# One block of a fused attention and expert kernel: ScalarE's queue put in another order

## The chip, the core and the metric

The kernel runs on one core of a Trainium2 chip. The core has a matrix engine (TensorE, PE in the profile), a vector engine (VectorE, DVE), an activation engine (ScalarE, ACT), GpSimd (POOL) and SyncE (SP), which here only issues DMA transfers. Each engine has its own list of instructions, works through it in order, and waits at an instruction until the semaphores that this instruction names have been raised by other engines or by a landed transfer. The metric is the device time of one launch in microseconds (us). Lower is better.

## What is computed

Three steps follow each other, on 2304 tokens of width 512:

```
scores = scale * q_c @ k_c.T                # attention in chunks of 64, 8 heads
attn   = exp(scores - max) / (sum + 1e-09)
x      = attn @ v_c
h = x @ w_in                                # first MLP, 512 -> 2048 -> 512
x = (h * clip(h + 3, 0, 6) / 6) @ w_out
...                                         # then top 2 of 8 experts, 512 -> 1024 -> 512 each
```

## The kernel before

**Precision by parts.** TensorE works on 32-bit values in a rounded format. To keep accuracy each operand is held as a rounded part ("hi") and a remainder ("lo"), and a product takes three passes: hi by hi, hi by lo, lo by hi. ScalarE makes each hi (a copy that rounds), VectorE makes the matching lo (value minus hi).

**Blocks and units.** The first MLP is done in five blocks of 4, 3, 4, 4 and 3 token tiles of 128 (`BT`). A block runs over `U1 = 16` units of 128 hidden columns. In unit u TensorE makes the first product (`mlp_s1`, L310, 12 matmuls), then the second product of the unit before (`mlp_o`, L322, 12 matmuls). Between the two stand four instructions that are called the chain of the activation here: ScalarE's relu (`mlp_r`, L351), VectorE's minimum and product (L352), ScalarE's copy g hi (`mlp_g`, L356), VectorE's remainder g lo (`mlp_lo`, L364).

**The first block does more.** `block0` is the only block in which the MLP's weights come as raw 64-bit words and have to be made into hi and lo. Each unit has two halves, one of `w_in` and one of `w_out`, of 512 KB raw. In unit u the half a = 2u+4 (unit u+2's `w_in`) and the half b = 2u+3 (unit u+1's `w_out`) are made: VectorE's shift `conv_1` (L160), merge `conv_2` (L167) and merge `conv_3` (L174), then ScalarE's copy `conv_hi` (L184), then VectorE's remainder `conv_lo` (L191). Raw halves land in three buffers (and for some early ones in spare room); `load_next` has SyncE load a further half when a `conv_3` has freed a buffer (L150). The remainder of half b is made one unit later, just behind L352: the code calls that half `late`.

In the same block the attention of tiles 4, 5 and 6 is done, each spread over four units, from unit 2, 6 and 10 on. I number these four units k = 0 to 3. In k = 0 the scores are there (`att_sc`); VectorE takes the maximum (`att_mx`, L211, L215) and ScalarE four of eight exponentials (`att_e`, L226). In k = 1 come the other four exponentials, VectorE's reciprocal of the sums (`att_r`, L236, L237) and four of eight scalings by it (`att_ns`, L250). In k = 2 come the other scalings. In k = 3 TensorE transposes (`att_pt`, L257), ScalarE copies that (`att_at`, L265), TensorE multiplies by v (`att_xo`, L278), and the result is split into hi (`att_hi`, L288) and lo (`att_lo`, L291). The next tile's q, k, v (768 KB) are loaded when `att_xo` is done (L119).

**What sets the order.** TensorE, VectorE and ScalarE are under a manual schedule: each engine's list is the order of the Python calls below. SyncE's transfers are placed by the scheduler.

Of the kernel before, what the change touches and what calls it, by code (L numbers as in the profile page):

```python
# [52 lines left out]
def tile_kernel(ctx, tc, qkv, w1u, w2u, wg, noise, out):  # L53
# [51 lines left out]
    late = tc.tile_pool(name="late", bufs=1)  # L105
# [56 lines left out]
    def conv_2(s):  # L162
        if s >= 2 * U1:
            return
        hi32 = st["raw64", s].rearrange("p (n c) -> p n c", c=2)[:, :, 1]
        u = st["u", s]
        nc.vector.scalar_tensor_tensor(u, hi32, -0x40000000, u, op0=ALU.bitwise_and, op1=ALU.bitwise_or)  # L167

    def conv_3(s):
        if s >= 2 * U1:  # L170
            return
        lo32 = st.pop(("raw64", s)).rearrange("p (n c) -> p n c", c=2)[:, :, 0]
        u = st["u", s]
        nc.vector.scalar_tensor_tensor(u, lo32, 29, u, op0=ALU.logical_shift_right, op1=ALU.bitwise_or)  # L174

    def load_next(*halves):
        for s in halves:
            load64(s + 7 if s < 10 else s + 3 if s >= 14 else -1)

    def conv_hi(s):  # L180
        if s >= 2 * U1:
            return
        j, h = divmod(s, 2)
        nc.scalar.activation(st["w", "m", j][:, 0, h * DM:(h + 1) * DM], st["u", s].bitcast(F32), AF.Copy)  # L184

    def conv_lo(s):
        if s >= 2 * U1:
            return
        j, h = divmod(s, 2)
        hi, lo = (st["w", "m", j][:, i, h * DM:(h + 1) * DM] for i in range(2))  # L190
        nc.vector.tensor_tensor(lo, st.pop(("u", s)).bitcast(F32), hi.bitcast(F32), op=ALU.subtract)  # L191
# [39 lines left out]
    def att_r(t, eng=None):  # L231
        eng = eng or nc.vector
        sm, su, mx, acts = st["att", t]
        if not acts:
            nc.vector.tensor_reduce(su, sm, axis=AX.X, op=ALU.add)
        eng.tensor_scalar(su, su, 1e-9, None, op0=ALU.add)  # L236
        nc.vector.reciprocal(su, su)  # L237
# [9 lines left out]
    def att_ns(t, heads):  # L247
        sm, su, mx, acts = st["att", t]
        for h in heads:
            nc.scalar.activation(sm[:, h], sm[:, h], AF.Copy, scale=su[:, h])  # L250
# [9 lines left out]
    def att_at(t, at, dve=False):  # L260
        dst, src = at.rearrange("p k n -> p (k n)"), st.pop(("pt", t))
        if dve:
            nc.vector.tensor_copy(dst, src)
        else:
            nc.scalar.activation(dst, src, AF.Copy)  # L265
        st["attT", t] = at
# [81 lines left out]
    def mlp_r(b, u):  # L348
        n = BT[b] * P
        r = work.tile([P, DM], F32, tag="r", bufs=2, name="r")[:, :n]  # L350
        nc.scalar.activation(r, st["h", b], AF.Relu, bias=b3)  # L351
        nc.vector.scalar_tensor_tensor(r, r, 6.0, st["h", b], op0=ALU.min, op1=ALU.mult)  # L352
        st["r", b] = r

    def mlp_g(b, u):
        nc.scalar.activation(st["g", b, u][:, 0], st["r", b], AF.Copy)  # L356
# [537 lines left out]
    def block0():  # L894
        nonlocal prev
        n0, lag = st.get("tick", 0), 2
        for i in range(BT[1]):
            k = n0 + 7 * (4 * i + lag)
            t = LT + i
            at(ticks, k + 3, att_sc, t)  # L900
            at(ticks, k + 20, att_pt, t)
            at(ticks, k + 24, att_xo, t)
        late = []
        for u in range(U1):
            t, k = LT + (u - lag) // 4, ((u - lag) % 4 if lag <= u < lag + 4 * BT[1] else None)
            b, a = 2 * u + 3, 2 * u + 4
            mlp_s1(0, u, gtile(), 0)
            mlp_r(0, u)
            if k == 3:
                att_at(t, at_[0])  # L910
            mlp_g(0, u)
            if u == 0:
                conv_3(1), conv_hi(1), conv_lo(2)
                load_next(1, 2)
                late = [1]
            else:
                conv_lo(*late)
            for pb, v in prev:
                mlp_o(pb, v)
            prev = [(0, u)]  # L920
            if k == 1:
                att_e(t, range(4, 8))
            elif k == 2:
                att_ns(t, range(4, 8))
            conv_1(a), conv_2(a)
            mlp_lo(0, u)
            if u == 0:
                conv_lo(*late)
            conv_1(b)
            conv_3(a), conv_hi(a)  # L930
            conv_2(b)
            if k == 0:
                att_mx(t, True)
            elif k == 1:
                att_r(t)
            elif k == 3:
                att_hi(t)
            conv_3(b), conv_hi(b)
            conv_lo(a)
            if k == 0:  # L940
                att_e(t, range(4))
            elif k == 1:
                att_ns(t, range(4))
            elif k == 3:
                att_lo(t)
                if t + 2 < NTILE:
                    load_tile(t + 2, bufs[4 + t % 2])
            late = [b]
            load_next(b, a)

    nxt = {"u": U1}
# [185 lines left out]
```

## Time and profile before

| what | us |
|---|---|
| median of three runs (lowest, highest) | 950.94 (950.82, 953.96) |
| the profiled execution's own time | 942.9 |
| its span, first to last instruction | 941.1 |
| TensorE busy in the span | 910.5 |
| VectorE busy | 480.6 |
| ScalarE busy | 332.4 |

The profiled execution is a launch of its own, so its rows add up to 942.9 and not to the median. Busy time is summed over the whole span; the first block's units lie between about 20 and 131 us of it, and what bounds them is read from that stretch alone.

### The profile page before, as it was taken

The numbers are of one execution on the slowest core, as the hardware profiler recorded it, in microseconds if no ns is written. First come the engines' busy times: TensorE is split into PE (matmuls) and PEld (weight loads), VectorE is DVE, ScalarE is ACT, GpSimd is POOL, SyncE is SP. The second block draws the span as 40 slices with busy tenths as digits, with TensorE's granted clock in tenths as the row PEclk, the third lists the DMA queues.
The fourth block names the chain that finished last, engine by engine and source line by source line (L and its number), as shares of the span: only waits on it lengthen the run. The fifth ranks groups of instructions, "written<-read, shape, count | busy, mean of one in ns | idle before, by whom it ended". The sixth has DMA issues, their size and how long they took to land. (4 is left out here: it accounts for less than half of the span.)

```text
span 941.1 us, 14415 instructions
## 1 busy us (share of the span) xinstructions
PE 910.5 (97%) x5804; PEld 766.3 (81%) x5804; DVE 480.6 (51%) x912; ACT 332.4 (35%) x642; POOL 231.8 (25%) x214
## 2 busy tenths in 40 slices
PE   7988899999999999999999999999999999999996
PEld 4666678888777777788988898889898988888885
DVE  7888875463445344536553455444545444441321
ACT  5455543333323222344551443333333333321210
POOL 1000000011001000032202435763655446332311
PEclk9999999999999999999999999999999999999998
DMA  9625449322200610013640764563736445240412
GB/s 341 226 85 156 148 131 346 94 68 69 68 26 13 181 41 1 1 58 83 186 146 2 156 170 129 122 153 93 160 99 132 118 118 141 69 54 20 54 23 34
DMA packets 49916, 101.49 MB, mean 108 GB/s; under 512 B 17040, under 2 KB 23056, under 8 KB 49840
## 3 DMA queue, kind: packets, MB, share of 16 engines
q1 hardware_dynamic: 38736, 80.38, 27.2%
q0 software_dynamic: 11104, 20.10, 11.8%
q8 instruction: 47, 0.77, 0.4%
q14 instruction: 29, 0.24, 0.1%
HBM read 77.66 MB, written 22.75 MB: 107 GB/s over the span
## 5 line engine op out<-in xcount | busy, mean ns | idle before, releaser
L322 PE MATMUL bp<-w,g 128*128 128x512 f32 (+1 forms) x1812 | 456.7, 398 | 4.7 <-ACT g L356 3.4
L322 PEld LDWEIGHTS bp<-w,g 128*128 128x128 f32 (+1 forms) x1812 | 328.8, 186 | 81.2 <-ACT g L356 5.4
L310 PE MATMUL bp<-Xa,w 128*128 128x304 f32 (+3 forms) x1344 | 241.2, 330 | 2.1 <-ACT Xa L288 1.3
L310 PEld LDWEIGHTS bp<-Xa,w 128*128 128x128 f32 x1344 | 210.1, 188 | 24.8 <-ACT Xa L288 1.4
L583 POOL DMA_INDIRECT xrq<-x2d,iq x114 | 119.2, 1045 | 96.1 <-DVE iq L577 34.8
L626 DVE SCALAR_TENSOR_TENSOR g<-bp,g 128x304 fp32r<-128x304 f32 (+2 forms) x128 | 60.3, 471 | 130.9 <-ACT g L625 130.8
L139 DVE TENSOR_TENSOR w<-raw,w 128x1024 fp32r<-128x1024 f32 x64 | 78.4, 1226 | 89.2 <-ACT w L138 89.2
L548 POOL DMA_INDIRECT table<-pay,slot x36 | 36.2, 1006 | 339.3 <-DVE slot L545 329.9
L625 ACT ACTIVATE g<-bp 128x304 fp32r<-128x304 f32 (+2 forms) x128 | 54.2, 424 | 168.7 <-PE bp L310 168.5
L310 PE MATMUL bp<-Xb,w 128*128 128x384 f32 (+1 forms) x480 | 106.1, 366 | 0.0
L352 DVE SCALAR_TENSOR_TENSOR r<-r,bp 128x512 f32<-128x512 f32 (+1 forms) x80 | 50.7, 634 | 105.7 <-ACT r L351 105.3
L310 PE MATMUL bp<-Xe,w 128*128 128x304 f32 (+1 forms) x672 | 102.7, 308 | 0.0
L310 PEld LDWEIGHTS bp<-Xe,w 128*128 128x128 f32 x672 | 99.8, 188 | 3.3
L310 PEld LDWEIGHTS bp<-Xb,w 128*128 128x128 f32 x480 | 85.2, 188 | 12.5 <-issue 1.8
L653 POOL DMA_INDIRECT out_dram<-arena,tab x40 | 62.6, 1564 | 123.6 <-DVE arena L650 100.2
L138 ACT ACTIVATE w<-raw 128x1024 fp32r<-128x1024 f32 x64 | 67.7, 1058 | 59.3 <-PE bp L322 58.6
L351 ACT ACTIVATE r<-bp,b 128x512 f32<-128x512 f32 (+1 forms) x80 | 51.3, 641 | 105.6 <-PE bp L310 105.6
L364 DVE TENSOR_TENSOR g<-r,g 128x512 fp32r<-128x512 f32 (+1 forms) x80 | 50.9, 637 | 39.7 <-ACT g L356 39.5
L356 ACT ACTIVATE g<-r 128x512 fp32r<-128x512 f32 (+1 forms) x80 | 47.1, 589 | 57.3 <-DVE r L352 57.3
L184 ACT ACTIVATE w<-u 128x512 fp32r<-128x512 f32 x32 | 20.2, 632 | 47.0 <-DVE u L174 47.0
L401 DVE STREAM_TRANSPOSE arena<-xrq 128x512 f32<-128x512 f32 (+1 forms) x30 | 31.4, 1045 | 0.0
L767 POOL MEMSET zero<- 128x1024 f32 x1 | 1.0, 953 | 110.3 <-DMA arena<-in_qkv_dram 110.3
(150 smaller groups left out, 479.5 us busy)
## 6 DMA issues: line engine op xcount, KB each, us to landing
raw<-in_w2u_dram SPq DMA_DIRECT2D x64, 512.0 KB, 3.6
raw<-in_w1u_dram SPq DMA_DIRECT2D x24, 512.0 KB, 4.5
arena<-in_qkv_dram SPq DMA_DIRECT2D x14, 768.0 KB, 11.6
out_dram<-zero SPq DMA_DIRECT2D x4, 1536.0 KB, 10.7
rawx<-in_w1u_dram SPq DMA_DIRECT2D x8, 512.0 KB, 3.7
x2d<-x SPq DMA_DIRECT2D x15, 256.0 KB, 2.2
xq<-x2d SPq DMA_DIRECT2D x44, 64.0 KB, 2.6
xrq<-x2d,iq POOLq DMA_INDIRECT x114, 2.9
```

Source lines behind the costliest of these rows:

```text
L138: nc.scalar.activation(w[:, 0], raw, AF.Copy)
L139: nc.vector.tensor_tensor(w[:, 1], raw, w[:, 0].bitcast(F32), op=ALU.subtract)
L310: nc.tensor.matmul(dst, w[:, a, kd * P:(kd + 1) * P], x[:, b, kd, t0:t0 + n], start=(k == 0), stop=(k == 3 * KD - 1))
L322: nc.tensor.matmul(acc[i][:gi.shape[2]], gi[:, a], w[:, b, DM:], start=(first and j == 0), stop=(last and j == 2))
L351: nc.scalar.activation(r, st["h", b], AF.Relu, bias=b3)
L352: nc.vector.scalar_tensor_tensor(r, r, 6.0, st["h", b], op0=ALU.min, op1=ALU.mult)
L356: nc.scalar.activation(st["g", b, u][:, 0], st["r", b], AF.Copy)
L364: nc.vector.tensor_tensor(g[:, 1], st["r", b], g[:, 0].bitcast(F32), op=ALU.subtract)
L583: nc.gpsimd.indirect_dma_start(out=xr[:, c * P:(c + 1) * P], out_offset=None, in_=x2q, in_offset=bass.IndirectOffsetOnAxis(ap=st["iq", key ...
L625: nc.scalar.activation(g[:, 0, t0:t0 + n], h, AF.Relu)
L626: nc.vector.scalar_tensor_tensor(g[:, 1, t0:t0 + n], h, 0.0, g[:, 0, t0:t0 + n].bitcast(F32), op0=ALU.max, op1=ALU.subtract)
L653: s = nc.gpsimd.indirect_dma_start(out=out, out_offset=bass.IndirectOffsetOnAxis(ap=tab[:n, i, 0:1], axis=0), in_=y, in_offset=None, compu ...
```

## The change

Only the order of calls in `block0` changes; no instruction is added or taken away.

- ScalarE's copy of the late half (`conv_hi(b)`) no longer stands at a unit's end, ahead of the next unit's relu. It stands behind that relu (and behind `att_at` in k = 3), ahead of g hi.
- The four exponentials of k = 0 and the four scalings of k = 1 that stood at the unit's end, behind `conv_hi(b)`, now stand behind `conv_hi(a)`, ahead of the next relu.
- On VectorE the maximum (k = 0) and the reciprocal (k = 1) move from behind to ahead of `conv_2(b)`, and the remainder of half a, `conv_lo(a)`, moves from behind to ahead of `conv_3(b)`.
- In unit 0 `conv_3(1)` and two loads are called earlier in the text.

```diff
-        late = []
+        late = 1
...
             mlp_r(0, u)
+            if u == 0:
+                conv_3(1)
+                load_next(1, 2)
             if k == 3:
                 att_at(t, at_[0])
+            if u > 0:
+                conv_hi(late)
             mlp_g(0, u)
             if u == 0:
-                conv_3(1), conv_hi(1), conv_lo(2)
-                load_next(1, 2)
-                late = [1]
+                conv_hi(1), conv_lo(2)
             else:
-                conv_lo(*late)
+                conv_lo(late)
...
             conv_3(a), conv_hi(a)
-            conv_2(b)
             if k == 0:
-                att_mx(t, True)
+                att_mx(t, True), att_e(t, range(4))
             elif k == 1:
-                att_r(t)
+                att_r(t), att_ns(t, range(4))
             elif k == 3:
                 att_hi(t)
-            conv_3(b), conv_hi(b)
-            conv_lo(a)
-            if k == 0:
-                att_e(t, range(4))
-            elif k == 1:
-                att_ns(t, range(4))
-            elif k == 3:
+            conv_2(b), conv_lo(a), conv_3(b)
+            if k == 3:
                 att_lo(t)
...
-            late = [b]
+            late = b
             load_next(b, a)
```

ScalarE's list, from unit 2 (k = 0) into unit 3 (k = 1). Buffer numbers are shown: w_546 and w_605 are units' weight tiles, u_547 is half a and u_551 half b of unit 2, r and g belong to the activation. Before:

```order
L184 ACTIVATE w_546<-u_547 128x512
L184 ACTIVATE w_485<-u_551 128x512
L226 ACTIVATE arena_94,su_558<-pair0_72,mx_556 128x64 x4
L351 ACTIVATE r_584<-bp3_411,b3_81 128x512
L356 ACTIVATE g_571<-r_584 128x512
```

And now:

```order
L184 ACTIVATE w_546<-u_547 128x512
L226 ACTIVATE arena_94,su_557<-pair0_72,mx_555 128x64 x4
L351 ACTIVATE r_583<-bp3_411,b3_81 128x512
L184 ACTIVATE w_485<-u_551 128x512
L356 ACTIVATE g_570<-r_583 128x512
```

The copy of half b (from u_551) went from ahead of the exponentials and the relu to behind both.

ScalarE's list from the end of unit 4 (k = 2) into unit 5 (k = 3). Before:

```order
L184 ACTIVATE w_660<-u_661 128x512
L184 ACTIVATE w_605<-u_665 128x512
L351 ACTIVATE r_690<-bp3_411,b3_81 128x512
L265 ACTIVATE at0_100<-pair0_72 128x512
L356 ACTIVATE g_673<-r_690 128x512
```

And now:

```order
L184 ACTIVATE w_660<-u_661 128x512
L351 ACTIVATE r_689<-bp3_411,b3_81 128x512
L265 ACTIVATE at0_100<-pair0_72 128x512
L184 ACTIVATE w_605<-u_665 128x512
L356 ACTIVATE g_672<-r_689 128x512
```

The relu and the copy of the transposed tile now follow the copy of half a (u_661) directly.

VectorE's list at the end of unit 4, from `conv_3(a)` to the next unit's L352. Before:

```order
L174 SCALAR_TENSOR_TENSOR u_661<-rawx_120,u_661 128x512
L167 SCALAR_TENSOR_TENSOR u_665<-rawx_119,u_665 128x512
L174 SCALAR_TENSOR_TENSOR u_665<-rawx_119,u_665 128x512
L191 TENSOR_TENSOR w_660<-u_661,w_660 128x512
L352 SCALAR_TENSOR_TENSOR r_690<-r_690,bp3_411 128x512
```

And now:

```order
L174 SCALAR_TENSOR_TENSOR u_661<-rawx_120,u_661 128x512
L167 SCALAR_TENSOR_TENSOR u_665<-rawx_119,u_665 128x512
L191 TENSOR_TENSOR w_660<-u_661,w_660 128x512
L174 SCALAR_TENSOR_TENSOR u_665<-rawx_119,u_665 128x512
L352 SCALAR_TENSOR_TENSOR r_689<-r_689,bp3_411 128x512
```

The remainder of half a (L191) and the last step of half b (the second L174) have changed places. The lists of TensorE, of GpSimd and of SyncE's transfers are as they were.

## Rows read from the trace of the kernel before

**Rows 1.** Busy time by engine in two stretches; PEclk is the granted clock.

```profile
29.00:125.00 96.00, 83.39 (x517) 62.80 (x516) 80.61 (x149) 49.03 (x132) 0.50 (x1) 0.98 0.48 146
125.00:900.00 775.00, 773.58 (x4777) 662.11 (x4776) 369.04 (x696) 264.96 (x453) 220.93 (x196) 1.00 0.37 98
```

**Rows 2.** TensorE's waits, 29 to 125 us: total, times, longest.

```profile
PE pair L278 <- ACT at L265: 4.5, 3, 1.5
...
PE bp L322 <- ACT g L356: 3.1, 4, 1.9
```

**Rows 3.** VectorE's waits, 29 to 125 us.

```profile
DVE r L352 <- ACT r L351: 13.8, 11, 1.9
```

**Rows 4.** ScalarE's waits, 30 to 125 us; the view has no further rows.

```profile
ACT w L184 <- DVE u L174: 38.4, 27, 3.2
ACT g L356 <- DVE r L352: 8.3, 13, 0.8
```

**Rows 5.** VectorE's timeline in unit 8 (k = 2): start, duration, [idle before].

```profile
83.19 0.69 DVE L352 SCALAR_TENSOR_TENSOR r<-r,bp 128x512 f32<-128x512 f32 x1 [1.62 <-ACT r L351]
...
84.40 0.42 DVE L160 TENSOR_SCALAR u<-raw 128x512 int32<-128x512 int32 x1
...
86.40 0.68 DVE L174 SCALAR_TENSOR_TENSOR u<-raw,u 128x512 int32<-128x512 int32 x1
87.00 0.68 DVE L167 SCALAR_TENSOR_TENSOR u<-raw,u 128x512 int32<-128x512 int32 x1
87.71 0.69 DVE L174 SCALAR_TENSOR_TENSOR u<-raw,u 128x512 int32<-128x512 int32 x1
88.32 0.69 DVE L191 TENSOR_TENSOR w<-u,w 128x512 fp32r<-128x512 f32 x1
89.68 0.69 DVE L352 SCALAR_TENSOR_TENSOR r<-r,bp 128x512 f32<-128x512 f32 x1 [0.67 <-ACT r L351]
```

**Rows 6.** ScalarE's timeline at the same place.

```profile
88.44 0.63 ACT L184 ACTIVATE w<-u 128x512 fp32r<-128x512 f32 x1 [0.70 <-DVE u L174]
88.98 0.67 ACT L351 ACTIVATE r<-bp,b 128x512 f32<-128x512 f32 x1
89.55 0.59 ACT L265 ACTIVATE at<-pair 128x512 f32<-128x512 f32 x1
```

**Rows 7.** VectorE's timeline: L352 of units 1, 2, 6 and 13.

```profile
31.80 0.69 DVE L352 SCALAR_TENSOR_TENSOR r<-r,bp 128x512 f32<-128x512 f32 x1 [0.68 <-ACT r L351]
...
38.30 0.69 DVE L352 SCALAR_TENSOR_TENSOR r<-r,bp 128x512 f32<-128x512 f32 x1 [0.67 <-ACT r L351]
...
67.23 0.69 DVE L352 SCALAR_TENSOR_TENSOR r<-r,bp 128x512 f32<-128x512 f32 x1
...
119.22 0.69 DVE L352 SCALAR_TENSOR_TENSOR r<-r,bp 128x512 f32<-128x512 f32 x1 [0.67 <-ACT r L351]
```

**Rows 8.** VectorE's timeline in unit 2 (k = 0), the maximum.

```profile
42.71 0.68 DVE L211 TENSOR_REDUCE mx<-pair 128x8 f32<-128x512 f32 x1
43.43 0.17 DVE L215 TENSOR_SCALAR mx<-mx 128x8 f32<-128x8 f32 x1
```

**Rows 9.** ScalarE's timeline, units 2 and 3: exponentials up to the relu, and the scalings.

```profile
44.77 0.30 ACT L226 ACTIVATE arena<-pair,mx 128x64 f32<-128x64 f32 x1
...
45.92 0.70 ACT L351 ACTIVATE r<-bp,b 128x512 f32<-128x512 f32 x1
...
52.59 1.05 ACT L250 ACTIVATE arena<-arena,su 128x64 f32<-128x64 f32 x4
```

**Rows 10.** The raw halves' transfers (L150), 60 to 130 us.

```profile
DMA to landing us min/median/max: 3.7/4.1/4.5
```

**Rows 11.** VectorE's timeline: the one wait for a raw half, in unit 10.

```profile
97.98 0.43 DVE L160 TENSOR_SCALAR u<-raw 128x512 int32<-128x512 int32 x1 [0.51 <-DMA raw<-in_w1u_dram]
```

**Rows 12.** TensorE's timeline: the last L278 of the block, and the slow matmuls of unit 3.

```profile
48.05 4.64 PE L322 MATMUL bp<-w,g 128*128 128x512 f32 x12 [1.89 <-ACT g L356]
...
119.73 0.69 PE L278 MATMUL pair<-at,arena 64*64 64x64 f32 x32 [1.50 <-ACT at L265]
```

More of the change, by code (lines that the diff above doesn't have):

```diff
@@ L927, in block0 @@
             if u == 0:
-                conv_lo(*late)
+                conv_lo(1)
             conv_1(b)
             conv_3(a), conv_hi(a)
-            conv_2(b)
             if k == 0:
-                att_mx(t, True)
+                att_mx(t, True), att_e(t, range(4))
             elif k == 1:
-                att_r(t)
+                att_r(t), att_ns(t, range(4))
             elif k == 3:
                 att_hi(t)
-            conv_3(b), conv_hi(b)
-            conv_lo(a)
-            if k == 0:
-                att_e(t, range(4))
-            elif k == 1:
-                att_ns(t, range(4))
-            elif k == 3:
+            conv_2(b), conv_lo(a), conv_3(b)
+            if k == 3:
                 att_lo(t)
```

## The prediction

> **What bounds the kernel now.** I read first where TensorE stands idle. From 125 to 900 us it is busy for 773.58 of 775 us [rows 1]: nothing but fewer or faster matmuls would shorten that stretch, and whatever the first block saves is carried to the end. From 29 to 125 us, which is the first block, TensorE is busy for 83.39 of 96, so 12.6 us are there to be won. The view of its waits says for whom: the transposed tile (L265) and g hi (L356), both from ScalarE [rows 2]. The last such wait ends at 119.73, before L278 of unit 13 [rows 12]; how much earlier that row comes is the result.
>
> ScalarE itself is busy for only 49.03 of the 96 us [rows 1]. Its own waits name VectorE alone, 38.4 us of them at the weight copy; no wait for a product of TensorE is in the view [rows 4]. So the relu, which needs a product, never waited for it: it waited in its queue. VectorE is busy for 80.61 of 96 us [rows 1] and waits 13.8 us for the relu, 11 times [rows 3]. Rows 5 and 6 show one such wait. VectorE begins the last step of half b at 87.71. ScalarE's copy of it begins at 88.44, then the relu at 88.98, and VectorE's L352 begins at 89.68 after 0.67 us of nothing. VectorE waits for an instruction that stands behind a copy that waits for VectorE. That circle is the bound of this block.
>
> **The change, step by step.** From rows 5 and 6: a copy begins 0.73 after the start of the VectorE step that feeds it; its result can be used 0.67 later (0.63 long, and some 0.03 to be seen, as between the relu's end at 89.65 and L352); ScalarE takes a next copy 0.54 after the last; VectorE's steps follow each other 0.60 apart (0.71 where one needs the one before). Count a unit from its L352. In unit 8 the first shift stands at 1.21, conv_3(a) at 3.21, conv_2(b) at 3.81, and the next L352 at 6.49 [rows 5].
>
> *A unit without attention on VectorE (k = 2; unit 1).* Now conv_lo(a) follows conv_2(b). The copy of half a is usable at 3.21 + 1.40 = 4.61, so conv_lo(a) begins there and not at 4.41; conv_3(b) at 5.21, L352 at 5.81, since the relu stands ready. The copy of half b is usable 1.40 after conv_3(b), which is 0.80 into the next unit; the late remainder would begin at 0.60 there and loses 0.20 in units whose predecessor is of this kind. That is 5.81 against 6.49.
>
> *k = 0.* The maximum costs 0.72 and the small step behind it 0.08 (0.17 long, less the overlap) [rows 8]. It ends at 3.21 + 0.60 + 0.72 + 0.17 = 4.70, the exponentials begin at 4.74 and last 1.15 (44.77 to 45.92) [rows 9], so the relu begins at 5.89 and L352 at 6.60. VectorE alone would be there at 6.41.
>
> *k = 1.* The copy of half a begins at 3.94, the scalings at 4.48; they take 0.95 (1.05 less the overlap) [rows 9]. Relu at 5.43, L352 at 6.13. VectorE's two small steps lie inside that.
>
> *k = 3.* 5.81, plus 0.20 for the late remainder, plus 0.60 for att_lo: 6.61.
>
> *Unit 0's end and unit 1.* L352 of unit 1 no longer waits (0.68) [rows 7]: 0.68 earlier. Unit 1 itself takes 5.81 + 0.20 = 6.01 and took 38.30 - 31.80 = 6.50: 0.49.
>
> *Units 2 to 5.* 6.80 (with 0.20 from unit 1) + 6.13 + 5.81 + 6.61 = 25.35, before 67.23 - 38.30 = 28.93 [rows 7]: 3.58.
>
> *Units 6 to 12, where the raw halves come late.* From unit 7 on half a of a unit is loaded into the buffer that conv_3(a) of the unit before has freed, so shorter units leave the transfer less room. The load is issued 0.73 after conv_3(a) starts (as the copy is) and lands 3.7 later at best [rows 10]: 4.46 with the wake-up. After k = 0 the next shift comes 6.60 - 3.21 + 1.21 = 4.60 later: no wait. After k = 1: 4.13, a wait of 0.33. After k = 2: 5.81 - 3.21 + 1.41 = 4.01, a wait of 0.45. After k = 3 the tile's 768 KB go ahead of it. Before, in unit 10, the shift was due 6.49 - 3.21 + 1.21 = 4.49 after conv_3(a) and came 0.60 later (0.51 idle, plus overlap) [rows 11], so at 5.09; now it would be due 6.61 - 3.21 + 1.21 = 4.61 less 0.20 that k = 3 loses ahead of conv_3(a) = 4.41: 0.68. The lengths are 6.60, 6.13, 6.14 (5.81 and 0.33), 7.06 (6.61 and 0.45), 7.28 (6.60 and 0.68), 6.13 and 6.14, in sum 45.48; before, 119.22 - 67.23 = 51.99 [rows 7]: 6.51.
>
> *Unit 13.* Before, the relu, L265 and L278 followed the copy of half b, and L278 began at 119.73, 0.51 after L352 [rows 7, 12]. Now the relu follows the copy of half a: conv_3(a) + 0.73 + 0.54 for the relu, + 0.57 for L265 (88.98 to 89.55), + 0.63 for it to end and be seen [rows 6] = 2.47 after conv_3(a), which is 2.60 ahead of L352. L278 begins 0.13 ahead of L352: 0.64 more.
>
> The sum is 0.68 + 0.49 + 3.58 + 6.51 + 0.64 = 11.9 us. Issues of DMAs keep their order on SyncE's queue, and unit 0's two loads follow the same conv_3 as before. The copy of half b now stands ahead of g hi. I cost that at nothing: g hi waits for L352 anyway (0.73 after its start), and the copy, which begins 0.13 after L352 does, is off ScalarE 0.06 before that. Without this cover it is 0.54 a unit. TensorE must be able to follow: of the 96 us it could give up 12.6 of idle time and, if it is not slowed again, some 2.3 of the 4.64 us that the matmuls at 48.05 took [rows 12], so its floor is some 81 us and I ask for 84.1.
>
> What the transfers will take is not shown for loads packed this closely. From below, no load waits more than before: 0.33 + 0.45 + 0.33 + 0.17 come back (the last is 0.68 less the 0.51 there is), 13.2 us in sum. From above, every load takes the longest shown, 4.5 [rows 10]: 0.8 later in units 8, 9 and 12 and, less the 0.14 of room that k = 0 leaves, 0.66 in units 7 and 11 (unit 10's price holds the tile's transfer already), 3.7 in sum: 8.2 us. I take 3.7, since the load that matters is issued after a long pause of SyncE.
>
> A page of the Trainium skill prices the transfer: DMA: Bandwidth & Descriptors, section Anatomy of one DMA, has about 2.0 us plus the bytes over 436e3 per us, which is an estimate of 3.2 us for 512 KB (the fit is given for transfers that GpSimd issues). By it the load would be there after 3.96, the waits behind k = 1 and k = 2 would be gone and the gain 13.0 us, a time of 937.9. No row here shows it: the shortest of these landings is 3.7 [rows 10], and the sum goes by that.
>
> The profiled execution's 942.9 would become 931.0. The median of the runs stands 8.0 above that execution; I carry this difference over: 950.94 - 11.9 = 939.0.
>
> **Rivals.**
> *The raw halves bind.* All loads as slow as the slowest: 8.2 us, 942.7. For it: one wait already stands in the trace, and the buffers are only three. Against: it stands behind a 768 KB transfer.
>
> *TensorE's clock falls.* The granted clock of the block is 0.98 [rows 1]: the matmuls at 48.05 took 4.64 us at the lower level (1.2 GHz), right after 1.89 us of waiting [rows 12]. It cost nothing then, since VectorE was behind. With TensorE nearly bound, each fall costs up to 2.3 us; two make 943.6. Against: by the sum TensorE waits less, and the 1.5 us waits at L278 shrink. The Trainium skill's page TensorE: Matmul & The Clock Gate, section The HAM clock gate, has the throttled clock as the default that activity lifts; the trace agrees in that the one fall followed the longest wait.
>
> *Nothing is gained.* The relu may find its product late once it is early in the queue; VectorE then waits for TensorE in place of ScalarE. The floor above speaks against it: to lose 8 of the 11.9 us TensorE would need 92 us where it has 83.39 of work. With loads and clock both against it some 4 us would be left: 947, within 0.5%.
>
> *Slower.* The copy of half b now stands between the relu and g hi. If L352 is not what g hi waits for, g hi comes 0.54 later in each of 14 units, 7.6 us, and if TensorE then waits for g hi each time (it does so in 4 cases now) [rows 2] with no relu wait saved, the time is 958.5. It decides from the point where the copy begins more than 0.2 after L352, so if the relu itself comes late. Rows 4 show no late product.
>
> **How the numbers follow.** My forecast has 0.66, slow loads 0.14, the clock 0.09: all three faster by over 0.5% (4.75 us, about what a measurement of this kernel can tell from no change), 0.89 in sum. Nothing gained has 0.07, slower 0.04. The predicted time is that of the first, 939.0. The range goes from the transfers' lower bound (937.7) less half of the 3.1 us by which the runs differ, to slow loads (942.7) with half a fall of the clock (1.2): 936.0 to 944.0. It leaves out some 0.2.
>
> **What would show it.** VectorE's waits for the relu in the first block should fall from 13.8 us to about 1.2 (0.2 in each k = 0 and k = 1). New waits should be at L191 for the copies (about 0.2 each) and at L160 for raw halves (near 1.8 us in sum, in units 8 to 12). L352 should come at about 62.5 in unit 6 and 108.0 in unit 13; the last L278 that waits at about 107.8. TensorE's work after it should be the old one, moved. If L351 waits for L310, the third rival is right; if the L160 waits exceed 4 us, the first; if PEclk is under 1.00 in more than one place, the second. The prediction is wrong if L278 of unit 13 has not come 10 us earlier.

## The result and the profile after

The changed kernel takes 939.46 us (median of five runs, 935.81 to 940.00) where the kernel before took 952.66 beside it (950.82 to 956.03): a ratio of 0.985, with a 95% interval of [0.982, 0.988]. That is faster by 1.5%, three times the 0.5% named in the prediction. The forecast was 939.0.

I read the profile after in the order in which the prediction read the one before. First the busy time by engine, of the changed kernel's first block and of the stretch behind it (columns as in [rows 1]):

```profile
29.00:115.00 86.00, 82.92 (x528) 64.04 (x527) 82.00 (x151) 49.31 (x133) 0.96 (x1) 1.00 0.53 165
...
125.00:900.00 775.00, 768.82 (x4735) 657.25 (x4734) 360.50 (x683) 259.05 (x444) 220.76 (x195) 0.99 0.37 98
```

In the block TensorE and VectorE are now busy for 82.92 and 82.00 of 86 us: the circle that kept both waiting is gone, and both are close to full. The second row holds a surprise: behind the block, where nothing was changed, TensorE is busy for 4.8 us less than in [rows 1]. The last experiments are about that.

VectorE's waits in the changed kernel, 29 to 115 us; these two rows answer to the one in [rows 3]:

```profile
DVE u L160 <- DMA raw<-in_w1u_dram: 0.9, 3, 0.4
DVE r L352 <- ACT r L351: 0.8, 4, 0.2
```

The wait for the relu fell from 13.8 us to 0.8. A small wait for raw halves is new. TensorE's waits in the same kernel, 29 to 118 us:

```profile
PE pair L203 <- DVE Xb L291: 1.0, 2, 0.6
PE pair L278 <- ACT at L265: 0.9, 3, 0.5
PE bp L322 <- DVE g L364: 0.8, 2, 0.4
```

The 4.5 us before L278 and the 3.1 us for g hi in [rows 2] have become 0.9 us and nothing. The same view of the kernel before, 29 to 125 us, has a third large wait for ScalarE, which the prediction passed over:

```profile
PE pair L257 <- ACT arena L250: 3.3, 3, 1.4
```

It stood for the scaled exponentials and is gone too. Of the waits that are left 1.8 us name VectorE and 0.9 ScalarE. ScalarE's waits in the changed kernel, 30 to 115 us:

```profile
ACT w L184 <- DVE u L174: 32.8, 21, 3.1
ACT g L356 <- DVE r L352: 2.4, 8, 0.6
ACT arena L226 <- DVE mx L215: 0.7, 3, 0.3
```

ScalarE still waits 33 us for VectorE's merges, almost as long as in [rows 4]. That costs nothing, because nothing that VectorE needs stands behind these waits any more. VectorE's timeline of the changed kernel at unit 9 (k = 3), to be held against [rows 5]:

```profile
81.72 0.68 DVE L352 SCALAR_TENSOR_TENSOR r<-r,bp 128x512 f32<-128x512 f32 x1
82.50 0.69 DVE L191 TENSOR_TENSOR w<-u,w 128x512 fp32r<-128x512 f32 x1
...
85.30 0.68 DVE L174 SCALAR_TENSOR_TENSOR u<-raw,u 128x512 int32<-128x512 int32 x1
85.90 0.69 DVE L167 SCALAR_TENSOR_TENSOR u<-raw,u 128x512 int32<-128x512 int32 x1
86.69 0.69 DVE L191 TENSOR_TENSOR w<-u,w 128x512 fp32r<-128x512 f32 x1
87.30 0.68 DVE L174 SCALAR_TENSOR_TENSOR u<-raw,u 128x512 int32<-128x512 int32 x1
87.90 0.68 DVE L291 TENSOR_TENSOR Xb<-pair,Xb 128x512 fp32r<-128x512 f32 x1
88.50 0.68 DVE L352 SCALAR_TENSOR_TENSOR r<-r,bp 128x512 f32<-128x512 f32 x1
```

And ScalarE's timeline at the end of that unit, to be held against [rows 6]:

```profile
86.02 0.64 ACT L184 ACTIVATE w<-u 128x512 fp32r<-128x512 f32 x1 [2.95 <-DVE u L174]
86.56 0.58 ACT L288 ACTIVATE Xb<-pair 128x512 fp32r<-128x512 f32 x1
87.04 0.68 ACT L351 ACTIVATE r<-bp,b 128x512 f32<-128x512 f32 x1
88.02 0.63 ACT L184 ACTIVATE w<-u 128x512 fp32r<-128x512 f32 x1 [0.30 <-DVE u L174]
89.21 0.63 ACT L356 ACTIVATE g<-r 128x512 fp32r<-128x512 f32 x1 [0.57 <-DVE r L352]
```

The relu is now over at 87.72, 0.78 before VectorE takes it at 88.50. The copy of half b (88.02) runs behind the relu and is done 0.56 before g hi begins. Both steps that the prediction priced at 0.20 are there: the late remainder begins 0.78 after L352 in place of 0.60 (82.50 after 81.72), and the remainder of half a 0.79 after the merge ahead of it (86.69 after 85.90), a stall too short for the view to list it. At the end of that unit there is room between the copy of half b and g hi. At its start there is next to none; ScalarE's timeline there:

```profile
81.84 0.63 ACT L184 ACTIVATE w<-u 128x512 fp32r<-128x512 f32 x1 [0.30 <-DVE u L174]
82.44 0.63 ACT L356 ACTIVATE g<-r 128x512 fp32r<-128x512 f32 x1
```

The copy begins 0.12 after L352 (81.72) and g hi 0.72 after it, as in the prediction (0.13 and 0.73).

TensorE's timeline of the changed kernel, the last L278 of the block that waits and the first product of the second block. The latter is my mark for the end of the first block; in the profile before it stands at 131.54.

```profile
107.30 0.69 PE L278 MATMUL pair<-at,arena 64*64 64x64 f32 x32 [0.21 <-ACT at L265]
...
119.12 1.21 PE L310 MATMUL bp<-Xb,w 128*128 128x384 f32 x6
```

L278 came 12.43 us earlier than in [rows 12] and the mark 12.42: the block gave 12.4 us, where 11.9 were forecast. Yet the profiled execution took 939.69 us, where the prediction had 931.0 for it and the one before took 942.9: only 3.2 less. The other 9.2 us are in the unchanged part, and TensorE's waits between 500 and 600 us show where:

```profile
PE bp L310 <- DVE g L626: 4.0, 2, 2.1
```

It waits twice for VectorE's g in the expert stage (L626), which the profile before does not have, and between the two waits a stretch of 10.2 us at half the clock begins (the windows row of 560 to 580 us):

```profile
560.00:580.00 20.00, 16.02 (x72) 13.87 (x71) 8.46 (x12) 5.27 (x9) 7.92 (x8) 0.74 0.28 84
```

The second wait (2.1 us) lies inside that stretch, so TensorE works for 8.1 us of it at half the clock and loses 4.0 us by that. With the 4.0 us of the two waits that is 8.0 us; the same view has 0.9 us more in short waits than the view before (1.1 for 0.6 at L610, 0.4 at L322). Either the change caused this, or the 951 us that most runs of the kernel before take contain it too and its profiled execution happened not to.

### The profile page after: what moved, and what is told of

Its sections match the earlier page's. It is cut to its first block, busy times and chain, and to the rows that moved or that the text cites. A ratio compares the mean times of both kernels' runs of the same rounds, so it can differ in the third digit from the quotient of the medians.

```text
span 937.9 us, 14420 instructions
## 1 busy us (share of the span) xinstructions
PE 912.2 (97%) x5804; PEld 768.6 (82%) x5804; DVE 480.1 (51%) x912; ACT 331.0 (35%) x642; POOL 232.1 (25%) x214
## 5 line engine op out<-in xcount | busy, mean ns | idle before, releaser
L322 PE MATMUL bp<-w,g 128*128 128x512 f32 (+1 forms) x1812 | 456.2, 397 | 1.6 <-DVE g L364 0.8
L322 PEld LDWEIGHTS bp<-w,g 128*128 128x128 f32 (+1 forms) x1812 | 329.1, 186 | 76.8 <-DVE g L364 3.0
L310 PE MATMUL bp<-Xa,w 128*128 128x304 f32 (+3 forms) x1344 | 241.2, 330 | 2.1 <-ACT Xa L288 1.3
L310 PEld LDWEIGHTS bp<-Xa,w 128*128 128x128 f32 x1344 | 210.1, 188 | 24.7 <-ACT Xa L288 1.4
L626 DVE SCALAR_TENSOR_TENSOR g<-bp,g 128x304 fp32r<-128x304 f32 (+2 forms) x128 | 60.0, 472 | 139.6 <-ACT g L625 112.8
L310 PE MATMUL bp<-Xe,w 128*128 128x304 f32 (+1 forms) x672 | 105.4, 312 | 4.0 <-DVE g L626 4.0
L310 PEld LDWEIGHTS bp<-Xe,w 128*128 128x128 f32 x672 | 101.8, 192 | 8.0 <-DVE g L626 4.8
L310 PE MATMUL bp<-Xb,w 128*128 128x384 f32 (+1 forms) x480 | 106.1, 366 | 0.0
L310 PEld LDWEIGHTS bp<-Xb,w 128*128 128x128 f32 x480 | 85.3, 188 | 12.5 <-issue 1.8
L352 DVE SCALAR_TENSOR_TENSOR r<-r,bp 128x512 f32<-128x512 f32 (+1 forms) x80 | 50.6, 633 | 85.3 <-ACT r L351 76.0
L351 ACT ACTIVATE r<-bp,b 128x512 f32<-128x512 f32 (+1 forms) x80 | 51.3, 642 | 98.2 <-PE bp L310 90.7
L364 DVE TENSOR_TENSOR g<-r,g 128x512 fp32r<-128x512 f32 (+1 forms) x80 | 51.0, 637 | 39.7 <-ACT g L356 38.2
```

The costliest lines, as they stand in the source:

```text
L310: nc.tensor.matmul(dst, w[:, a, kd * P:(kd + 1) * P], x[:, b, kd, t0:t0 + n], start=(k == 0), stop=(k == 3 * KD - 1))
L322: nc.tensor.matmul(acc[i][:gi.shape[2]], gi[:, a], w[:, b, DM:], start=(first and j == 0), stop=(last and j == 2))
L364: nc.vector.tensor_tensor(g[:, 1], st["r", b], g[:, 0].bitcast(F32), op=ALU.subtract)
L626: nc.vector.scalar_tensor_tensor(g[:, 1, t0:t0 + n], h, 0.0, g[:, 0, t0:t0 + n].bitcast(F32), op0=ALU.max, op1=ALU.subtract)
```

## The experiments

The theory is the circle of the prediction: VectorE's L352 waits for a relu that stands behind a copy that waits for VectorE. Its rivals are that the order of VectorE's own list gives the gain, that the exponentials and scalings ahead of the relu do, or that the clock does. The second question is the stretch near 560 us. The diffs are against the changed kernel. From here, *mark* is the time of the second block's first product in the profiled execution (before 131.54, changed 119.12). The four profiles of the changed kernel have it between 118.70 and 119.17, the two of the kernel before at 131.54 and 131.10, so differences of the mark under 0.5 us decide nothing.

| run | median us | before on that chip | ratio, 95% interval | mark |
|---|---|---|---|---|
| changed kernel again | 937.56 | 950.91 | 0.985 [0.983, 0.987] | 119.17 |
| ScalarE's new order alone | 940.78 | 950.91 | 0.989 [0.986, 0.991] | 121.29 |
| VectorE's new order alone | 957.95 | 950.91 | 1.007 [1.005, 1.010] | 141.19 |
| copy stays ahead of the relu | 947.38 | 950.91 | 0.996 [0.994, 0.998] | 128.52 |
| copy behind g hi | 945.63 | 943.07 | 1.003 [1.002, 1.004] | 134.02 |
| merge of half b first | 929.67 | 943.07 | 0.986 [0.984, 0.987] | 118.54 |
| buffer freed early | 929.98 | 943.07 | 0.986 [0.984, 0.988] | 119.37 |
| both of these | 930.87 | 943.07 | 0.987 [0.985, 0.989] | 119.74 |
| changed kernel, third time | 937.70 | 950.96 | 0.986 [0.984, 0.989] | 118.75 |
| merge of half b first, again | 936.60 | 950.96 | 0.985 [0.982, 0.987] | 118.75 |
| kernel before, again | 943.48 | 943.32 | 1.000 [0.999, 1.001] | 131.10 |
| changed kernel, fourth time | 941.07 | 958.25 | 0.984 [0.979, 0.988] | 118.70 |

**The changed kernel again.** No edit; it gives the spread and a reference on the chip of the next three.

> The changed kernel once more, to see how far one execution's time outside the first block moves. Mark: the start of the second block's first product on TensorE, 131.5 us before and 119.1 in the first profile of the changed kernel. If the first block's gain is the order of instructions, the mark stands at 119 again within 0.5 us, whatever the whole time does. If the time differs by several us from 939.7 while the mark stays, the difference lies behind the first block: I expect a wait of some us for the experts' raw weights and a fall of TensorE's clock near 560 us in the slower executions (granted clock 0.993) and neither in the faster (0.996). A rival holds the whole gain for chance in the clock: then the mark would move by some us from one profile to the next.

The mark repeats within 0.05 us (119.17), and so does the wait near 560 us: 4.6 us in two waits for L626. The rival of the clock asked for a mark that moves by some us, and it does not. Nor did the one fall of the clock in the block of the kernel before cost anything: unit 3, in which it lies, took 7.60 us, and so did unit 7, the next with k = 1, without a fall.

**ScalarE's new order alone.** VectorE's list is put back, ScalarE's stays as changed.

```diff
             conv_3(a), conv_hi(a)
+            conv_2(b)
             if k == 0:
-                att_mx(t, True), att_e(t, range(4))
+                att_mx(t, True)
             elif k == 1:
-                att_r(t), att_ns(t, range(4))
+                att_r(t)
...
-            conv_2(b), conv_lo(a), conv_3(b)
+            conv_3(b)
+            conv_lo(a)
+            if k == 0:
+                att_e(t, range(4))
+            elif k == 1:
+                att_ns(t, range(4))
```

> ScalarE's list as in the changed kernel, VectorE's as before (the maximum and the reciprocal behind conv_2(b), conv_3(b) ahead of conv_lo(a)). Theory of the circle: the relu no longer stands behind the copy, so most of the gain is there. A unit without attention takes 5.73 us (all steps, no wait), k = 0 takes 7.2 and k = 1 6.5, since the exponentials and scalings begin some 0.6 and 0.4 later and the relu follows them; raw halves cost about 2. L352 of unit 13 at about 109.4, mark at about 121: a gain of 10 to 11 us in the block. Rival, VectorE's own order makes the gain: the mark stays near 131.

The mark comes at 121.29: 10.3 of the 12.4 us are there without any move on VectorE. What is left is seen in VectorE's waits of this kernel, 29 to 118 us:

```profile
DVE r L352 <- ACT r L351: 4.3, 6, 0.8
DVE u L160 <- DMA raw<-in_w1u_dram: 1.2, 3, 0.6
```

The maximum stands behind conv_2(b) here, the exponentials wait for it and the relu stands behind them. The moves on VectorE are worth the other 2.2 us.

**VectorE's new order alone.** The reverse: ScalarE's copy of half b is back at the unit's end, ahead of the relu, and the exponentials behind it. The calls of unit 0 go back as well; they are not shown.

```diff
-            if u > 0:
-                conv_hi(late)
             mlp_g(0, u)
...
-                att_mx(t, True), att_e(t, range(4))
+                att_mx(t, True)
             elif k == 1:
-                att_r(t), att_ns(t, range(4))
+                att_r(t)
...
-            conv_2(b), conv_lo(a), conv_3(b)
-            if k == 3:
+            conv_2(b), conv_lo(a), conv_3(b), conv_hi(b)
+            if k == 0:
+                att_e(t, range(4))
+            elif k == 1:
+                att_ns(t, range(4))
+            elif k == 3:
```

> VectorE's list as in the changed kernel, ScalarE's as before (copy of half b at the unit's end, ahead of exponentials or scalings and the relu). Theory of the circle: conv_3(b) now ends 0.5 to 0.7 later in each unit and the copy, and the relu behind it, with it, so the 13.8 us of waits for the relu grow to about 22 and the block gets longer by about 7 us: mark at about 139, the whole some 0.7% slower than before. Rival, VectorE's own order makes the gain: the mark falls below 125.

It is slower than the kernel before, by 0.7% in the whole time and by 9.7 us at the mark (the profiled execution took 961.69 us, 3.7 more than the median). VectorE's timeline of this kernel, from the last step of half b to L352:

```profile
93.89 0.69 DVE L174 SCALAR_TENSOR_TENSOR u<-raw,u 128x512 int32<-128x512 int32 x1
95.84 0.69 DVE L352 SCALAR_TENSOR_TENSOR r<-r,bp 128x512 f32<-128x512 f32 x1 [1.27 <-ACT r L351]
```

And ScalarE's timeline there:

```profile
94.60 0.63 ACT L184 ACTIVATE w<-u 128x512 fp32r<-128x512 f32 x1 [1.36 <-DVE u L174]
95.14 0.67 ACT L351 ACTIVATE r<-bp,b 128x512 f32<-128x512 f32 x1
```

This is the circle with its cover taken away. In [rows 5] the remainder of half a stood between the last merge and L352 and filled 0.60 us of the way over ScalarE; here that work is done earlier, and VectorE stands idle for 1.27 instead of 0.67. From 29 us up to the mark VectorE waits 23.7 us for the relu, in 15 places, where the kernel before waits 15.1 in 12. So the two halves of the change don't add: VectorE's order is worth +9.7 us alone and -2.2 behind ScalarE's. Of the 9.7 us 8.8 are there at the last L352 of the block (139.63 for 130.87); the last 0.9 came behind it, where the granted clock was at half from about 128 to 131.5 us.

**The copy stays ahead of the relu.** Only the exponentials and the scalings move, ahead of the copy; conv_hi(b) stays at the unit's end, and VectorE's list (maximum, reciprocal, conv_lo(a)) is that of the kernel before. The calls of unit 0 go back as well; they are not shown.

```diff
             conv_3(a), conv_hi(a)
+            conv_2(b)
             if k == 0:
...
-            if u > 0:
-                conv_hi(late)
             mlp_g(0, u)
...
-            conv_2(b), conv_lo(a), conv_3(b)
+            conv_3(b), conv_hi(b)
+            conv_lo(a)
```

> From the kernel before, the exponentials of k = 0 and the scalings of k = 1 alone go ahead of the copy of half b; the copy stays ahead of the relu. Theory of the circle: the relu still waits about 0.7 us in each unit, but the 1.15 and 0.95 of the exponentials and scalings no longer stand behind that; six units gain 0.5 to 1, relu waits about 9.7 us, mark at about 128, 3 to 4 us earlier. Rival, that the exponentials in the relu's way are the whole cause: the mark falls to 122 or below and the waits to 6 or less.

The mark is at 128.52, 3.0 earlier than before, and VectorE still waits 10.7 us in 11 places for the relu (29 to 118 us; the kernel before has 13.1 in 10 there). Moving the attention's work off the unit's end is the smaller part.

**The copy behind g hi.** The copy goes one place further on: the relu is free, but now the late remainder has to wait for a copy that waits for L352.

```diff
+            mlp_g(0, u)
             if u > 0:
                 conv_hi(late)
-            mlp_g(0, u)
```

> From the changed kernel, ScalarE's copy of half b goes one place further back, behind g hi. My sum costs the copy's place ahead of g hi at nothing, since it fills the gap in which g hi waits for L352. Behind g hi it begins 1.27 after L352 instead of 0.13, so the late remainder on VectorE, 0.60 behind L352, waits until about 1.94: 1.1 to 1.3 more in each of 13 units. No relu wait returns, but the mark goes to about 133.5, later than before the change (131.5), and nearly all of the gain is gone. Rival, that it is enough to have the relu ahead of the copy: the mark stays within 1 us of 119.

All of the gain is lost and 2.5 us more (mark 134.02). VectorE's waits of this kernel, 29 to 118 us, name the new circle:

```profile
DVE w L191 <- ACT w L184: 14.6, 12, 1.2
DVE r L352 <- ACT r L351: 0.6, 3, 0.2
```

The wait for the relu is gone just as in the changed kernel, and a wait of the same size stands one instruction further down. TensorE's view of the kernel shows what that delays: 5.6 us in 7 waits for g lo (L364). So it is not enough that the relu goes first. Of the three places tried for the copy, only the one in which ScalarE waits for VectorE anyway, between relu and g hi, closes no circle.

**The merge of half b first.** This concerns the 0.20 us that the late remainder loses and the 0.20 of conv_lo(a).

```diff
-            conv_2(b), conv_lo(a), conv_3(b)
+            conv_2(b), conv_3(b), conv_lo(a)
```

> From the changed kernel, conv_3(b) goes back ahead of conv_lo(a) on VectorE; ScalarE's list and the place of the maximum and the reciprocal stay. By my steps the two remainders then find their copies ready: a unit without attention takes 5.73 and not 5.81 to 6.01, and the 0.2 at the late remainder goes; units 7 to 12 give some of it back to the raw halves, whose buffer is freed no earlier. Mark at about 118.3, 0.8 earlier than in the changed kernel, waits for raw halves somewhat longer (about 1.2 against 0.9). Rival, that putting conv_lo(a) first is part of the gain: the mark goes to 120 or later.

The mark was 118.54, with the block's start (L352 of unit 0) 0.9 later than in the changed kernel's first profile (the granted clock is 0.66 between 15 and 20 us here and 1.00 there), so 93.48 us from there to the mark where the changed kernel has 94.95. The repeat did not bear it out:

> e6's order (conv_3(b) ahead of conv_lo(a)) beside the changed kernel. From the first L352 to the second block's first product the profiles have 93.5 us in e6 against 94.7 and 95.0 in the two of the changed kernel: I expect it 1.2 to 1.5 us (0.15%) faster than the changed kernel, which is less than the intervals of the ratios so far (0.2 to 0.3% to each side), so that it may not show in them; the same stretch of the profile should be 93.5 again. Rival, that e6's stretch was a chance of its transfers: it is within 0.3 of the changed kernel's in this profile.

There it takes 94.58 from L352 of unit 0 (24.17) to the mark (118.75), and the changed kernel beside it 94.32 (24.43 to 118.75); VectorE waits 1.8 us for raw halves. In whole time the two differ by 1.1 us (936.60 and 937.70) with overlapping intervals. Over the four profiles of the changed kernel the same stretch takes 94.3 to 95.0. Whether this order is better by up to 1 us stays open.

> The changed kernel and e6's order on one chip, since the runs so far stand against different runs of the kernel before (943.1 in one set, 950.9 in the other, where every profile but the first has TensorE waiting twice and a fall of its clock near 560 us). If the block's gain of 12.4 us is all there is, this kernel is 12.4 us faster than the kernel before on this chip whichever level that has: a ratio of 0.9869 at 943 or 0.9870 at 951. If something behind the block gains as well, the ratio is 0.985 again.

In that profile VectorE waits for no raw half at all, and 1.1 us in 6 places for the relu.

**The buffer freed early.** conv_3(a) goes right behind conv_2(a), which frees the raw buffer earlier (in unit 9 conv_3(a) begins 2.57 after L352 in place of 3.58).

```diff
             conv_1(a), conv_2(a)
+            if u > 0:
+                conv_3(a), conv_hi(a)
             mlp_lo(0, u)
...
-            conv_3(a), conv_hi(a)
+            if u == 0:
+                conv_3(a), conv_hi(a)
```

> From the changed kernel, conv_3(a) and the copy of half a go directly behind conv_2(a), ahead of g lo and conv_1(b), so that its raw buffer is free and the next half a is loaded some 0.8 earlier. If the raw halves' landing is what units 8 to 10 still wait for, the waits for them go from 0.9 to about 0; but the merge now follows the step it needs without a gap (0.72 for 0.60). Mark between 118.5 and 119.1. Rival, raw halves bind everywhere: the mark goes to 117 or below.

The waits for raw halves are gone, as meant, but the mark (119.37) is not earlier. VectorE's timeline of this kernel shows where it went:

```profile
83.95 0.69 DVE L167 SCALAR_TENSOR_TENSOR u<-raw,u 128x512 int32<-128x512 int32 x1
84.68 0.69 DVE L174 SCALAR_TENSOR_TENSOR u<-raw,u 128x512 int32<-128x512 int32 x1
85.29 0.68 DVE L364 TENSOR_TENSOR g<-r,g 128x512 fp32r<-128x512 f32 x1
```

The two merges of one half, now neighbours, start 0.73 apart in place of 0.60, and g lo comes 3.18 after its L352 (82.11) where in the changed kernel it comes 2.64 after it (84.36 and 81.72). By the gap of the merges a unit without attention takes 5.96 (unit 12), where the changed kernel's takes 5.83. TensorE's waits of this kernel, 29 to 118 us:

```profile
PE bp L322 <- DVE g L364: 2.5, 4, 1.2
```

**Both.** The last two edits together.

> conv_3(b) ahead of conv_lo(a) and conv_3(a) directly behind conv_2(a), on top of the changed kernel. The waits that my steps know are then gone (relu, copies, raw halves), and the mark should be at 118.0 to 118.5, about 1 us earlier than in the changed kernel and 13 earlier than before; TensorE's own work in the block (some 81 us of 96) leaves room for no more than 2 or 3 us beyond that.

VectorE has no wait left from 29 to 118 us, and still the mark is at 119.74, not 118.0 to 118.5. The block began 1.03 us later here (L352 of unit 0 at 25.20, with the granted clock at 0.66 between 15 and 20 us), but from there to the mark it takes 94.54 us, which the changed kernel takes too. VectorE's timeline of this kernel in unit 8 (k = 2) shows what takes the time:

```profile
76.64 0.68 DVE L352 SCALAR_TENSOR_TENSOR r<-r,bp 128x512 f32<-128x512 f32 x1
...
78.30 0.69 DVE L167 SCALAR_TENSOR_TENSOR u<-raw,u 128x512 int32<-128x512 int32 x1
79.02 0.69 DVE L174 SCALAR_TENSOR_TENSOR u<-raw,u 128x512 int32<-128x512 int32 x1
...
82.63 0.68 DVE L352 SCALAR_TENSOR_TENSOR r<-r,bp 128x512 f32<-128x512 f32 x1
```

The two merges of half a, and those of half b in the same way, are neighbours now and start 0.72 apart in place of 0.60. So the unit takes 5.99 without any wait, where the changed kernel's unit 12 takes 5.83. The expectation for the last edit had counted this gap for half a; the one for both left it out. TensorE waits 2.2 us for g lo here; what that costs beside the longer list was not separated. I had taken VectorE's waits for the bound once more, where the length of its list was.

**The stretch near 560 us.** In the runs so far the kernel before took 951 on the chips of the first four and of the third time, and 943 on the chip of the four in between. The next run was to show the kernel before at 951, with its profile.

> The kernel of before, unchanged. Its first profiled execution took 942.9 us while the median of its runs was 951, and no wait of TensorE near 560 us stood in it; the profiles of the changed kernel have two waits of 1.4 to 2.8 us there with a stretch at half clock. Theory: those waits are no part of the change, and the runs of before at 951 have them too. Then a profiled execution of about 951 has TensorE's waits at L310 for VectorE's L626 near 575 us and a half-clock stretch behind them, and one of about 943 has neither. In both, the first block is as before: L352 of unit 13 at 119.2, the second block's first product at 131.5. Rival: the changed order causes the waits. Then this profile has none, whatever its time, and 951 comes from elsewhere. The ratio to before is 1.00 by both.

It fell on a chip where the kernel takes 943, and there both theories leave it without waits near 560 us; it has none. Its block is as in the first profile (mark 131.10). One more run was made with the changed kernel.

> The changed kernel, unchanged. The kernel of before took 943 us on the chip where its profiles show no wait near 560 us and 951 on the other. Theory: the block gives 12 to 12.5 us on either, and what lies near 560 us adds its own 6 to 9 us on one chip only. Then where before takes 943 the changed kernel takes 930.5 to 931.5, with no wait of TensorE between 540 and 600 us; where before takes 951 it takes 937 to 939.5, with some. Rival: the changed order brings the waits near 560 us about. Then it takes 937 to 939 where before takes 943 too, and the waits are in its profile.

The last run fell on a chip where the kernel before takes 958.25, so what was asked, the changed kernel itself where before takes 943, was not met; its own time of 941.07 is above both ranges. What tells the rivals apart are all profiles together. First the windows row of 540 to 600 us of the buffer freed early, on a chip with 943:

```profile
540.00:600.00 60.00, 60.00 (x347) 53.72 (x346) 30.68 (x44) 22.19 (x35) 40.67 (x37) 1.00 0.51 132
```

Then the same row of the copy that stays ahead of the relu, on a chip with 951:

```profile
540.00:600.00 60.00, 55.18 (x312) 48.66 (x312) 29.00 (x42) 20.79 (x34) 28.19 (x27) 0.97 0.45 124
```

And of the changed kernel, fourth time, on the chip with 958:

```profile
540.00:600.00 60.00, 55.25 (x304) 48.28 (x303) 24.57 (x36) 17.20 (x28) 34.64 (x33) 0.97 0.42 112
```

On the two chips where the kernel before takes 943, none of the five kernels profiled, four of them with the relu first, has TensorE idle here (60.00 of 60). On the three chips with 951 to 958, all seven profiles have it idle for 2.5 to 5.2 us, the copy that stays ahead of the relu and VectorE's order alone too, which keep ScalarE's old order of copy and relu. So the order in the first block does not decide. The chip goes with it in all of them, but each chip stands for one batch of runs, so chip and batch are not told apart, and on one chip the idle time was 2.5 us in one profile and 5.0 in the next. That the kernel before has these waits where it takes 951 is likely but was not seen: both its profiles are of executions near 943 and without them.

## Why the prediction was right

**The bound.** It was the circle. ScalarE's order alone gave 10.3 of the 12.4 us; with the copy one place further on the same circle closed over L191 and all was lost; with VectorE's order alone it closed tighter.

**The terms.** The steps of the sum can be held against L352 of the units. Unit 1's came at 31.18 (0.62 earlier, 0.68 forecast). Unit 1 took 5.98 (6.01). Units 2 to 5 took 25.42 (25.35). Units 6 to 12, from 62.58 to L352 of unit 13 at 107.43, took 44.85 (45.48). L278 of unit 13 began 0.13 ahead of L352, as worked out. The marks of the forecast were 62.5, 108.0 and 107.8 for the L278, and are 62.58, 107.43 and 107.30.

**The mis-sized term** is the price of the raw halves, "near 1.8 us in sum, in units 8 to 12". The four profiles of the changed kernel have 0.9, 0.6, none and 0.6 us of it in all, and in the first only 0.6 of it lies in units 8 to 12. Counted as the sum counts it, by how much longer units 8, 9, 10 and 12 were than without these waits, the first has 1.07 us where 1.79 were forecast. There units 9, 10 and 12 took 6.78, 6.97 and 5.83 us where 7.06, 7.28 and 6.14 were forecast, and unit 8 took 6.32 for 6.14; with 0.09 more in unit 6 that is the whole difference of 0.63. I took 3.7 us, the shortest landing before [rows 10], for every load. Four rows of the changed kernel show that it was no single number: SyncE's issue of the load for unit 8 and VectorE's first step on it, and the same two for unit 12.

```profile
73.19 0.33 SPq L150 DMA_DIRECT2D raw<-in_w1u_dram  x1
...
77.11 0.43 DVE L160 TENSOR_SCALAR u<-raw 128x512 int32<-128x512 int32 x1 [0.42 <-DMA raw<-in_w1u_dram]
...
99.40 0.33 SPq L150 DMA_DIRECT2D raw<-in_w1u_dram  x1
...
102.82 0.43 DVE L160 TENSOR_SCALAR u<-raw 128x512 int32<-128x512 int32 x1
```

The first took 3.9 us, the second at most 3.4, since nothing waited for it. In unit 10, behind k = 3, 0.68 was forecast and 0.20 came, with the 768 KB of the tile ahead of it (issued at 86.02, used at 89.97). In the kernel with the buffer freed early the view gives the landings of this line from 60 to 118 us:

```profile
DMA to landing us min/median/max: 3.4/3.5/4.2
```

So at least half of the loads there were faster than the 3.7 us of the sum. Why one load takes 3.4 and another 3.9 stays open.

The estimate of 3.2 us from the Trainium skill's page DMA: Bandwidth & Descriptors, section Anatomy of one DMA, would leave no wait behind k = 1 and k = 2. The traces do not bear that out: the shortest landing is 3.4, and waits are there. Behind k = 1 three of the four profiles have one in unit 8 (0.42, 0.28 and 0.35 us) and none has one in unit 12; behind k = 2 one has it in unit 9 (0.18) and three in unit 13 (0.28, 0.18 and 0.24).

**The waits.** Relu 0.8 us (about 1.2 forecast; 1.1 in the third profile), the small stalls at L191 as priced, g hi late for nobody: the cover of the copy, 0.06 us by the prediction, held, with g hi 0.72 after L352 in unit 9 and 0.56 to spare at the end of that unit. The rival of a slower kernel asked that the copy begin more than 0.2 after L352; it began 0.12 after it in unit 9 and 0.48 ahead of it in the next unit (88.02 and 88.50). The rival of nothing gained asked for waits of L351 for L310; ScalarE's view has none. The clock was at 1.00 all through the block. Its rival was priced too high: the one fall in the kernel before lasted 3.4 us, so at half the clock it could cost at most 1.7 and not 2.3.

**The whole time.** The prediction carried the 8.0 us between the profiled execution (942.9) and the median (950.94) over as a plain difference. That gave the right whole time, but for a reason that it did not know: most likely the difference was the stretch of the unchanged part that takes longer in some batches of runs, for the kernels with the changed order have it too. That 939.0 came within 0.5 us of 939.46 is luck besides: the kernel before took 952.66 beside the changed one and not 950.94, and the gain was 13.2 and not 11.9, and these two differences cancel. The kernels with the new order show the same two levels: 930 us where the kernel before takes 943 (the merge of half b first, the buffer freed early), 937.6 (the changed kernel) where that takes 951. "TensorE's work after it should be the old one, moved" was wrong for the profile that came with the result, and the comparison of the two profiled executions alone (942.9 and 939.7) would have made the change look like a quarter of what it is.

In whole time the change is worth 13.2, 13.4 and 13.3 us in its first three comparisons, up to 1 us more than the 12.4 of the mark, and 17.2 in the fourth, where the runs of the kernel before lie between 953.22 and 960.89; where the difference to the mark lies was not found.

## What to carry to other kernels

When an engine with half its time free makes a full one wait, look at what stands ahead of the awaited instruction in its queue: if that waits for the full engine, the two form a circle, and the cure is to put the instruction that can run first, and the one that waits into a place where its engine waits anyway. Try the two engines' orders apart before judging them, since the one that looks like free tidying (VectorE's) cost 9.7 us by itself and gave 2.2 with the other. And take a place of the program that follows the change directly as the mark, not the end of the launch, when the profiled execution and the median differ.

## What the runs showed of the hardware

- One and the same kernel takes 943 us on two of the five chips of the experiments, 951 on two and 958 on one. In the profiles of the slower ones TensorE is idle for 2.5 to 5.2 us between 540 and 600 us, in waits that end 441 to 451 us behind the mark (563.5 and 574.8 us where the mark is at 119.12 and 128.52), so at one place of the program. In the first profile after, ScalarE's and VectorE's work for the activation of the experts is late there, after 4.54 and 4.48 us of idle time; why stays open. On the chip with 958 the idle time there is no longer (4.75 us), so the rest of its difference lies elsewhere.
- In each of these profiles the granted clock fell to half among or behind those waits, for 3.4, 6.8 or 10.2 us. Within the first block the kernel with VectorE's order alone fell to it four times for 3.4 us each (the waits there were up to 2.5 us), the kernel before once, and the changed kernel never. A fall need not cost anything. Two units of the kernel with VectorE's order alone, both with k = 2, the first with a fall in it and the second without:

```profile
57.22:64.37 7.15, 5.00 (x14) 3.51 (x14) 5.75 (x10) 3.45 (x9) 0.00 (x0) 0.76 0.07 26
88.69:95.84 7.15, 4.91 (x22) 3.33 (x20) 5.75 (x10) 3.46 (x9) 0.00 (x0) 1.00 0.35 121
```

Both take 7.15 us: where the circle of the two other engines sets the pace, TensorE has the time to be slow. Only the last of the four falls, at the end of the block, goes with a loss: the mark came 1.56 us behind the last L352, where it came 0.67 behind it before.
